# Eight units of the second attention layer on their first twelve key tiles, beside the last dense chain of the first layer

## The chip, the cores and the metric

The kernel runs on one core of one Trainium2 chip. The metric is device time in microseconds of one execution; lower is better. Three executions of the kernel before took 2576.21 to 2576.93 us, median 2576.77 us.

## The reference, cut to what matters

Two layers with the same weights, each one an attention block (32 heads of 16, one shared key and value head) and a dense block, each with a layer norm ahead and a residual sum behind. 2048 rows of 512.

```python
B, S, D, H = 1, 2048, 512, 32;  Dh = 16;  Dff = 1792
q = (x @ wq).reshape(B, S, H, Dh)...;  k = x @ wk;  v = x @ wv
scores = jnp.einsum("bhqd,bkd->bhqk", q, k) * (Dh ** -0.5)
p = _softmax(scores, axis=-1)
o = jnp.einsum("bhqk,bkd->bhqd", p, v)          # then heads joined, @ wo
h = jnp.maximum(jnp.einsum("bsd,df->bsf", x, w1), 0); return jnp.einsum("bsf,fd->bsd", h, w2)

x = x + A(layernorm(x)); x = x + B(layernorm(x))   # layer 0
x = x + A(layernorm(x)); x = x + B(layernorm(x))   # layer 1
```

## The kernel before, in words

**Units and steps.** A layer's rows are four blocks of 512 rows, its heads eight groups of four. A unit is one block with one group: units 0 to 31 are layer 0 (block 0 has units 0 to 7, and so on), units 32 to 63 layer 1. A unit runs over 16 key tiles of 128 keys; one unit on one key tile is a step, so there are 1024 steps. A step has two halves of scores (`scores`, line 709, two concurrent 64-row matmuls into one PSUM tile `st`), an exponential of 128 x 1024 behind each half on ScalarE (line 710), and one product with the values (`values`, line 715) which adds into the PSUM tile `acc`. There is one `acc` tile. When a run of consecutive steps of one unit ends, `keep` (line 718) copies `acc` to a tile `accs` in SBUF, or adds it there if the unit already has a sum. The program holds three tiles `p` of exponentials, so scores can lead products by three steps.

**What must come first.** A step of layer 1 on key tile kt needs the keys of block kt // 4 of layer 1, and those need the residual rows that the chain of layer 0 on that block makes. `chain(L, b)` (line 529) is that dense work: output projection, norm, the two dense products over 14 tiles of the hidden width, and for layer 0 the keys of layer 1 (`keys`, line 289). It can only start when the last unit of block b is done. `front` (line 926) asks for the keys with `until`; where they are not there yet, `until` (line 785) issues all the work that they wait for at once, with no step in between ("forced": full 128-row matmuls, line 98, instead of the 64-row pairs of line 119, and ScalarE takes over copies).

**Order of steps.** `order` (line 813): units 0 and 1 alternate in groups of four key tiles, 2 to 31 run whole, then units 32 and 33 run key tiles 0 to 11, then both run tiles 12 to 15, then 34 to 63 run whole. Step 512 is the first of layer 1.

**Who mixes steps and dense work.** `timed` (line 844) writes TensorE's order ahead of time: after each half of scores it chooses a product, the next scores, or a piece of dense work. How much dense work a step gets is `rate` (line 791): what is left of the work at the head of a list, divided by the steps left to its deadline. `follow` (line 942) puts a chain on the list with its size and its deadline as a step number. The chain of layer 0 on block 3 has size 414 and deadline 531; behind it come the queries of block 3 (`queries`, deadline 575) and those of blocks 1 and 2 (`late`, deadline 640).

**Queries of a unit.** `load_q` (line 663) brings a unit's queries from DRAM (`fqd`) into one of three SBUF tiles `fqop` by two DMAs on SP's queue; `after` (line 971) calls it when unit U has ended, for unit U + 2, behind `unit_out` (the sums' way to DRAM, `fod`). Queries get to DRAM in `queries`: per batch of two groups 12 DMAs of `fqd` (line 370), and per block eight more of `fqr` (line 350). SP's queue carries these, the weights `fw`, the sums (`fod`, `foraw`, `flsum`, `frd`, `frinv`, lines 731 to 754) and the residual rows, in the order of the program.

Of the kernel before, what the change touches and what calls it, by code (L numbers as in the profile page):

```python
# [44 lines left out]
class _Net:  # L45
# [333 lines left out]
    def start(self):  # L379
# [3 lines left out]
        def load(t):  # L383
            xs[t] = self.wt("xt", [P, D], bufs=6)
            self.nc.sync.dma_start(xs[t], self.x[0, t * P:(t + 1) * P, :])
# [44 lines left out]
    def residual(self, L, b):  # L430
        src = self.x[0, b * D:(b + 1) * D, :] if L == 0 else self.xres[b]
        xs = []
        for s in range(4):
            xt = self.wt("xt", [P, D], bufs=6)
            self.nc.sync.dma_start(xt, src[s * P:(s + 1) * P, :])
            xs.append(xt)
        return xs
# [91 lines left out]
    def chain(self, L, b):  # L529
# [33 lines left out]
        if self.early:  # L563
            for s in range(4):
                ps = self.early[s]
                for i, (x, y) in enumerate(self.out_parts(s, 3)):
                    nc.tensor.matmul(ps, x, y, start=False, stop=(i == 2))
                    yield 1.0
                added(s, ps)
                yield from alone(s)  # L570
        else:
            jobs = [([o for G in range(4) for o in self.out_parts(s, G)],
                     lambda ps, s=s: added(s, ps), lambda s=s: alone(s)) for s in range(4)]
            yield from self.batch(*jobs[0:2])
            yield from self.batch(*jobs[2:4])
        yield from self.flip(todo)
# [86 lines left out]
    def load_q(self, U):  # L663
        nc = self.nc
        L, b, u = U // 32, (U // 8) % 4, U % 8
        self.until(lambda: self.haveq[L, b] > u // 2)
        q = self.qop[U % 3]
        r = 48 if self.exact else 49
        for h in range(2):
            nc.sync.dma_start(_f(q)[64 * h:64 * h + r], self.qd[L, b][u, h, 0:r])  # L670
        return q
# [46 lines left out]
    def keep(self, U, acc):  # L718

        if U not in self.sums:  # L720
            self.sums[U] = self.wt("accs", [P, D], bufs=1 if self.exact else 2)
# [35 lines left out]
    def unit_norm(self, U):  # L757
        nc = self.nc
        o, r = self.ol
        G = (U % 8) // 2  # L760
        h, l = self.ot2[0][:, G], self.ot2[1][:, G]
# [51 lines left out]
    def order(self):  # L813
# [4 lines left out]
        out += [(U, kt) for U in (32, 33) for kt in range(12)] + [(U, kt) for U in (32, 33) for kt in range(12, KT)]  # L818
        return out + [(U, kt) for U in range(34, 64) for kt in range(KT)]
# [88 lines left out]
    def run(self):  # L908
        self.normed, self.todo = (1, 3), []
        self.have, self.haveq = [0, 0], {(L, b): 0 for L in range(2) for b in range(NB)}  # L910
        self.gens, self.lag, self.left, self.spent, later = [], 0, 0.0, 0.0, {}
        self.setup()
        self.add(self.start(), 200, 29)
        qs = {U: self.load_q(U) for U in range(2)}
# [6 lines left out]
        steps = self.order()  # L921
        n = len(steps)
        accs, ps, self.sums = {}, {}, {}
        self.first = lambda i: i == 0 or steps[i - 1][0] != steps[i][0]

        def front(i):
# [3 lines left out]
            if self.exact and kt == 0:  # L930
                self.row_max(L, qs[U])
            ps[i] = self.wt("p", [P, 4, D], bufs=3)
            self.scores(U, kt, qs[U], ps[i], 0)

        def back(i):
            U, kt = steps[i]
            self.scores(U, kt, qs[U], ps[i], 1)
# [4 lines left out]
        def follow(L, b):  # L942
            if L == 0 and b == NB - 1:
                self.add(self.chain(L, b), 414, 531)
                self.add(self.queries(1, 3, range(4)), 52, 575)
                self.add(self.late(1, (1, 2)), 114, 640)
            else:
                i0 = 128 * (4 * L + b + 2) + (5 if (L, b) == (0, 2) else 0)
                self.add(self.chain(L, b), (466 if b == 0 else 414) if L == 0 else 390, i0 + (2 if (L, b) != (1, 2) else -6))
# [21 lines left out]
        def after(i):  # L971
            U, kt = steps[i]
            if kt == KT - 1:
                self.unit_out(U)
                if U + 2 < 64:
                    qs[U + 2] = self.load_q(U + 2)
# [100 lines left out]
```

## Time and profile before

| | us |
|---|---|
| median of 3 executions | 2576.77 |
| the profiled execution | 2580.33 |
| its span, first to last instruction | 2578.5 |
| TensorE busy | 2433.6 |
| ScalarE busy | 1992.6 |
| VectorE busy | 722.8 |
| GpSimd busy | 211.9 |

The profiled execution is 1.8 us longer than its span, and 3.6 us longer than the median. A busy time is the union of an engine's instructions; matmuls are pipelined and their ends are modelled, so a busy TensorE is not one at its peak. "PE" is TensorE's matmuls, "PEld" its weight loads, "ACT" ScalarE, "DVE" VectorE, "POOL" GpSimd, "SPq" SyncE's queue of DMA issues.

### The profile page before, as it was taken

The page shows a single profiled execution, that of the slowest core. Times are in us where ns is not written, and L with a number is a line of the kernel's source. Part 1 is how long each engine was busy: PE and PEld are TensorE (multiplying, and loading weights), DVE is VectorE, ACT ScalarE, POOL GpSimd, SP SyncE. Part 2 cuts the span into 40 slices and gives each one's busy share as a digit, 9 for nine tenths or more (in the row PEclk, how much of TensorE's full clock was granted, in tenths as well). Part 3 has the DMA queues.
Part 4 walks back from the last instruction along what each step waited for, and adds up shares of the span by engine and source line. Part 5 has one row for each costly group of instructions (what it writes and reads, how often), then busy time and mean ns, then how long its engine had stood idle before and what let it go on. Part 6 is the DMA issues. An engine that isn't in the chain of part 4 may idle for free.

```text
span 2578.5 us, 44807 instructions
## 1 busy us (share of the span) xinstructions
PE 2433.6 (94%) x18945; PEld 816.8 (32%) x18945; DVE 722.8 (28%) x1554; ACT 1992.6 (77%) x2114; POOL 211.9 (8%) x291
## 2 busy tenths in 40 slices
PE   6898999999999999999898999999999999999978
PEld 2222223333333333333243222233333333333324
DVE  4444423123231132111333132231113121221232
ACT  5487898878888888888542998888898888888830
POOL 2234530000000000000000010000000000000000
PEclk8899999999999999999899999999999999999989
DMA  2034442101311112120221121211112110221031
GB/s 87 22 111 130 131 131 73 52 29 41 98 56 50 40 36 78 41 68 29 82 70 36 48 71 48 86 57 61 35 67 67 56 48 28 77 66 57 21 114 64
DMA packets 110340, 165.12 MB, mean 64 GB/s; under 512 B 19872, under 2 KB 39600, under 8 KB 110128
## 3 DMA queue, kind: packets, MB, share of 16 engines
q1 hardware_dynamic: 110128, 162.16, 19.5%
q8 instruction: 150, 2.46, 0.4%
q14 instruction: 62, 0.51, 0.1%
HBM read 116.20 MB, written 45.88 MB: 63 GB/s over the span
## 4 chain that ended last, share of the span: by engine, by line
PE 77%; ACT 10%; DVE 5%; DMA 3%; issue 2%; POOL 2%; SPq 1%; ACTq 0%; POOLq 0%; DVEq 0%
PE facc L715 32%; PE fmisc L119 20%; PE fst L709 17%; ACT fp L710 10%; PE fmisc L98 7%; DVE fxtl L279 1%; PE fmisc L275 1%; DVE fbst L255 1%; SPq L370 1%; DMA flsum<-fod 1%; DVE fxt L508 1%; DVE fxth L93 1%; POOL fbmv L259 1%; DMA frinv<-frd 0%; DVE fxn L264 0%
## 5 line engine op out<-in xcount | busy, mean ns | idle before, releaser
L710 ACT ACTIVATE fp<-fst 128x1024 f32<-128x1024 f32 x2048 | 1947.7, 1029 | 363.6 <-PE fst L709 345.1
L715 PE MATMUL facc<-fp,fva 128*32 128x512 f32 x8192 | 1038.2, 604 | 11.9 <-DVE faccs L722 11.6
L709 PE MATMUL fst<-fqop,fkop 64*128 64x512 f16 x4096 | 785.2, 383 | 47.0 <-ACT fp L710 33.3
L709 PEld LDWEIGHTS <-fkop 64*128 64x128 f16 x4096 | 257.5, 93 | 875.9 <-issue 728.0
L715 PEld LDWEIGHTS facc<-fp,fva 128*32 128x32 f32 x8192 | 202.6, 108 | 409.5 <-issue 354.3
L119 PE MATMUL fmisc<-fxth,fw 64*128 64x512 f16 x1376 | 237.7, 376 | 2.3 <-DVE fseen L126 1.7
L119 PE MATMUL fmisc<-fw,fhh 64*128 64x512 f16 x1328 | 222.3, 376 | 3.6 <-DVE fseen L126 1.8
L508 DVE SCALAR_TENSOR_TENSOR fxt<-fmisc,fxt 128x512 f32<-128x512 f32 x156 | 103.2, 684 | 370.7 <-PE fmisc L119 319.9
L258 POOL TENSOR_SCALAR fbmv<-fbmv 128x1 f32<-128x1 f32 x84 | 22.2, 264 | 1867.5 <-DVE fbmv L257 1866.1
L126 DVE COPY fseen<-fmisc 1x1 f32<-1x1 f32 x236 | 25.4, 142 | 474.2 <-PE fmisc L119 474.2
L119 PEld LDWEIGHTS <-fw 64*128 64x128 f16 x2064 | 104.7, 94 | 96.1 <-issue 7.2
L119 PE MATMUL fmisc<-fxtl,fw 64*128 64x512 f16 x688 | 132.3, 376 | 0.2
L119 PE MATMUL fmisc<-fw,fhl 64*128 64x512 f16 x664 | 128.5, 376 | 0.0
L722 DVE COPY faccs<-facc 128x512 f32<-128x512 f32 x64 | 44.2, 691 | 275.5 <-PE facc L715 275.5
L587 DVE TENSOR_SCALAR fhh<-fmisc 128x512 f16<-128x512 f32 x84 | 57.6, 686 | 209.5 <-PE fmisc L119 209.5
L585 ACT ACTIVATE fhh<-fmisc 128x512 f16<-128x512 f32 x28 | 16.6, 597 | 100.9 <-PE fmisc L98 95.7
L588 DVE SCALAR_TENSOR_TENSOR fhl<-fmisc,fhh 128x512 f16<-128x512 f32 x112 | 77.4, 692 | 60.6 <-ACT fhh L585 57.7
L119 PEld LDWEIGHTS <-fhh 64*128 64x128 f16 x1328 | 68.8, 94 | 64.4 <-issue 12.8
L275 PE MATMUL fmisc<-fident,fxn 128*128 128x128 f32 x336 | 58.3, 308 | 31.6 <-DVE fxn L264 27.9
L98 PE MATMUL fmisc<-fw,fhh 128*128 128x512 f16 x232 | 69.0, 379 | 0.0
L98 PE MATMUL fmisc<-fxth,fw 128*128 128x512 f16 x208 | 64.1, 385 | 0.7 <-ACT fxth L91 0.7
L255 DVE BATCH_NORM_STATS2 fbst<-fxt 128x6 f32<-128x512 f32 x84 | 57.7, 687 | 17.6 <-DMA fxt<-in_A_x_dram 12.5
(132 smaller groups left out, 1299.8 us busy)
## 6 DMA issues: line engine op xcount, KB each, us to landing
fw<-fwd SPq DMA_DIRECT2D x224, 256.0 KB
fod<-faccs SPq DMA_DIRECT2D x64, 256.0 KB
fqop<-fqd SPq DMA_DIRECT2D x128, 98.0 KB
fxt<-in_A_x_dram SPq DMA_DIRECT2D x44, 256.0 KB
fqd<-fqh SPq DMA_DIRECT2D x128, 64.0 KB
foraw<-fod SPq DMA_DIRECT2D x32, 256.0 KB
frinv<-frd SPq DMA_DIRECT2D x32, 256.0 KB
fwraw<-in_B_w_dram SPq DMA_DIRECT2D x28, 256.0 KB
```

Source lines behind the costliest of these rows:

```text
L93: self.nc.vector.tensor_copy(out, ps)
L98: self.nc.tensor.matmul(ps, a, b, start=(i == 0), stop=(i == n - 1))
L119: mm(ps[j], a[r], b[r], start=(turn == 0 and i == 0), stop=(turn == 1 and i == n - 1), skip_group_check=True)
L255: nc.vector.bn_stats(st, xt)
L275: nc.tensor.transpose(ps[:, c * P:(c + 1) * P], xn[:, c * P:(c + 1) * P], self.ident)
L508: self.nc.vector.scalar_tensor_tensor(xt, ps, 1.0 / factor, xt, op0=MUL, op1=ADD)
L587: nc.vector.tensor_scalar(hh, ps, 0.0, None, op0=MAX)
L588: nc.vector.scalar_tensor_tensor(hl, ps, 0.0, _f(hh), op0=MAX, op1=SUB)
L709: nc.tensor.matmul(st[:, hf], self.kop[U // 32][h, kt * P:(kt + 1) * P], q[h, pr, :], start=True, stop=True)
L710: nc.scalar.activation(p[:, 2 * pr:2 * pr + 2], st, AF.Exp, scale=self.up ** -2)
L715: self.nc.tensor.matmul(acc[32 * j:32 * j + 32], self.va[U // 32][:, kt], p[:, 2 * pr + hf], start=start, stop=stop, skip_group_check=True)
L722: self.nc.vector.tensor_copy(self.sums[U], acc)
```

## The change

Units 32 to 39 now all run key tiles 0 to 11 (96 steps, 512 to 607), then all run tiles 12 to 15 (32 steps, 608 to 639). Their partial sums wait in SBUF, so `accs` has nine tiles. A unit's queries are loaded once for each run, at the end of the run two before it, and ahead of `unit_out`. The last chain of layer 0 gets the deadline 604, and what stands behind it 617, 632 and 648; `late(1, (1, 2))` becomes two entries. The chain of layer 0 on block 2 gets the deadline 510 (it was 519). `unit_norm` does not overwrite the attention output before the chain ahead has read it (`outs`, `asked`). `xt` has eight tiles instead of six.

```diff
-            xs[t] = self.wt("xt", [P, D], bufs=6)
+            xs[t] = self.wt("xt", [P, D], bufs=6 if self.exact else 8)
...
+        self.outs += 1
         yield from self.flip(todo)
...
-        q = self.qop[U % 3]
+        q = self.qop[self.loaded % 3]
+        self.loaded += 1
...
-            self.sums[U] = self.wt("accs", [P, D], bufs=1 if self.exact else 2)
+            self.sums[U] = self.wt("accs", [P, D], bufs=1 if self.exact else 9)
...
+        self.until(lambda: self.outs == self.asked)
...
-        out += [(U, kt) for U in (32, 33) for kt in range(12)] + [(U, kt) for U in (32, 33) for kt in range(12, KT)]
-        return out + [(U, kt) for U in range(34, 64) for kt in range(KT)]
+        out += [(U, kt) for kts in (range(12), range(12, KT)) for U in range(32, 40) for kt in kts]
+        return out + [(U, kt) for U in range(40, 64) for kt in range(KT)]
...
+        self.first = lambda i: i == 0 or steps[i - 1][0] != steps[i][0]
+        units = [steps[i][0] for i in range(n) if self.first(i)]
...
+        qs = {r: self.load_q(units[r]) for r in range(2)}
...
+            self.asked += 1
             if L == 0 and b == NB - 1:
-                self.add(self.chain(L, b), 414, 531)
-                self.add(self.queries(1, 3, range(4)), 52, 575)
-                self.add(self.late(1, (1, 2)), 114, 640)
+                self.add(self.chain(L, b), 414, 604)
+                self.add(self.queries(1, 3, range(4)), 52, 617)
+                self.add(self.late(1, (1,)), 57, 632)
+                self.add(self.late(1, (2,)), 57, 648)
             else:
-                i0 = 128 * (4 * L + b + 2) + (5 if (L, b) == (0, 2) else 0)
-                self.add(self.chain(L, b), (466 if b == 0 else 414) if L == 0 else 390, i0 + (2 if (L, b) != (1, 2) else -6))
+                early = {(0, 2): 2, (1, 2): 6}.get((L, b), -2)
+                self.add(self.chain(L, b), (466 if b == 0 else 414) if L == 0 else 390, 128 * (4 * L + b + 2) - early)
...
+            r = run_of[i] + 2
+            if (i + 1 == n or self.first(i + 1)) and r < len(units):
+                qs[r] = qs[r - 2] if units[r] == U else self.load_q(units[r])
             if kt == KT - 1:
                 self.unit_out(U)
-                if U + 2 < 64:
-                    qs[U + 2] = self.load_q(U + 2)
```

What the change does to the order is seen at three places.

**TensorE, where the last chain of layer 0 runs.** Before, at step 535: the last scores (`fst`), three products in a row (`facc`, x12), and behind them dense rows alone (`fw` weights, `fmisc` PSUM) until the keys are there, 324 of them full matmuls of line 98.

```order
L709 MATMUL fst_13017<-fqop_89,fkop_76 128x512
L709 LDWEIGHTS fkop_76
L709 MATMUL fst_13017<-fqop_89,fkop_76 128x512
L715 MATMUL facc<-fp,fva_78 32x512 x12
L119 LDWEIGHTS fw_12564
L119 MATMUL fmisc<-fxth,fw_12564 128x512
L119 LDWEIGHTS fw_12568
```

After, at step 550, in unit 35's first run (line 711 is 709 before, 717 is 715):

```order
L119 LDWEIGHTS fw_13164
L119 MATMUL fmisc<-fxtl,fw_13164 128x512
L711 LDWEIGHTS fkop_76
L711 MATMUL fst_13395<-fqop_91,fkop_76 128x512
L711 LDWEIGHTS fkop_76
L711 MATMUL fst_13395<-fqop_91,fkop_76 128x512
L717 MATMUL facc<-fp,fva_78 32x512 x12
L711 LDWEIGHTS fkop_76
L711 MATMUL fst_13413<-fqop_91,fkop_76 128x512
L711 LDWEIGHTS fkop_76
L711 MATMUL fst_13413<-fqop_91,fkop_76 128x512
L119 LDWEIGHTS fw_13168
```

The dense rows now stand between the two halves of a step's scores and behind them, and products come in groups of up to three. In all the order has 68, 100, 136, 128, 148, 188, 96 and 96 rows of line 119 in the eight stretches of 16 steps from 512 on, where it had 78, 104, 34, 24, 36, 60, 28 and 64 and the 324 full ones; the chain ends in step 607 with 16 rows of line 119, 16 transposes and the 12 matmuls of `keys` that no step stands between. From 640 to 767 it has 828 rows of line 119, where it had 736.

**SyncE's queue, in the runs of four steps.** Before, from the end of the second query batch of block 3 (`fqd13`) on, the next queries loaded (`fqop1`) are for a run that begins 16 steps later:

```order
L370 DMA fqd13_100<-fqh_14244 4x16x512 x2
L370 DMA fqd13_100<-fql_14245 4x16x512
L370 DMA fqd13_100<-fqh_14244 4x16x512
L350 DMA fqd13_100<-fqr_14317 4x512 x8
L435 DMA fxt_14327<-fxr1_102 128x512
L435 DMA fxt_14329<-fxr1_102 128x512
L435 DMA fxt_14331<-fxr1_102 128x512
L435 DMA fxt_14333<-fxr1_102 128x512
L731 DMA fod_14070<-faccs_14352 128x512
L670 DMA fqop1_90<-fqd10_97 49x1024 x2
```

After, from the end of the same batch on:

```order
L370 DMA fqd13_100<-fql_15277 4x16x512
L370 DMA fqd13_100<-fqh_15276 4x16x512
L672 DMA fqop2_91<-fqd10_97 49x1024 x2
L733 DMA fod_15304<-faccs_13380 128x512
L350 DMA fqd13_100<-fqr_15325 4x512 x8
L435 DMA fxt_15335<-fxr1_102 128x512
L435 DMA fxt_15337<-fxr1_102 128x512
L435 DMA fxt_15339<-fxr1_102 128x512
L435 DMA fxt_15341<-fxr1_102 128x512
L754 DMA frd_15356<-flsum_15239 128x32
L756 DMA frinv_15358<-frd_15356 128x1x512
L672 DMA fqop0_89<-fqd10_97 49x1024 x2
```

`fqop2` here holds the queries of unit 36, whose run begins at step 624, four steps behind the last matmul of the batch; `fqop0` those of unit 37 for step 628. The queries of unit 34, for step 616, stand in the same way behind the first batch, which ends in step 612.

**SyncE's queue, before unit 40.** In step 637 the order now has the second half of block 1's queries forced (24 rows of line 119 and four of line 343 with no step between), since the load of unit 40's queries asks for them. After:

```order
L370 DMA fqd11_98<-fqh_15794 4x16x512 x2
L370 DMA fqd11_98<-fql_15795 4x16x512
L370 DMA fqd11_98<-fqh_15794 4x16x512
L350 DMA fqd11_98<-fqr_15811 4x512 x8
L672 DMA fqop0_89<-fqd11_98 49x1024 x2
L733 DMA fod_15823<-faccs_14535 128x512
```

`fqop0` is unit 40's, for step 640. Before, block 1's queries went to DRAM 24 steps and more before that step.

## Rows read from the trace of the kernel before

**Rows 1.** the page, part 1: busy us (share of the span) and instructions of each engine
```profile
PE 2433.6 (94%) x18945; PEld 816.8 (32%) x18945; DVE 722.8 (28%) x1554; ACT 1992.6 (77%) x2114; POOL 211.9 (8%) x291
```

**Rows 2.** the page, part 5: the exponentials of a step on ACT
```profile
L710 ACT ACTIVATE fp<-fst 128x1024 f32<-128x1024 f32 x2048 | 1947.7, 1029 | 363.6 <-PE fst L709 345.1
```

**Rows 3.** busy time by stretch: PE, PEld, DVE, ACT, POOL, granted clock, DMA share, GB/s
```profile
982.70:1259.30 276.60, 260.44 (x2127) 89.91 (x2123) 69.27 (x152) 215.28 (x229) 8.27 (x17) 0.97 0.14 45
1259.30:1614.90 355.60, 337.42 (x2357) 109.07 (x2357) 99.81 (x195) 256.09 (x275) 24.89 (x43) 0.98 0.19 61
1614.90:1898.10 283.20, 275.98 (x2296) 91.04 (x2297) 62.17 (x137) 243.12 (x256) 5.43 (x10) 1.00 0.17 55
1235.70:1257.90 22.20, 12.40 (x47) 5.61 (x45) 11.76 (x26) 3.95 (x6) 4.34 (x8) 0.71 0.09 36
1315.60:1386.70 71.10, 70.49 (x342) 31.80 (x339) 22.16 (x36) 8.25 (x14) 1.13 (x3) 1.00 0.25 81
1386.70:1403.00 16.30, 8.83 (x34) 4.16 (x33) 9.46 (x19) 2.98 (x5) 3.79 (x6) 0.79 0.09 35
```

**Rows 4.** four stretches of 16 steps each, dense matmuls of line 119 alone
```profile
427.94:465.24 37.30, 18.18 (x135) 6.53 (x132) 1.00 0.27 85
1583.40:1614.90 31.50, 9.57 (x66) 3.04 (x62) 1.00 0.13 41
1930.50:1966.30 35.80, 9.58 (x72) 3.35 (x68) 1.00 0.14 43
1966.30:2001.50 35.20, 15.08 (x114) 5.46 (x110) 1.00 0.27 90
```

**Rows 5.** the third of them, transposes of line 275 alone
```profile
1930.50:1966.30 35.80, 2.41 (x16) 1.70 (x16) 1.00 0.14 43
```

**Rows 6.** chain of waits, 1185 to 1230 us: start, us, what: value products
```profile
1190.96 2.71 PE facc L715 x24
...
1196.48 0.99 PE facc L715 x8
```

**Rows 7.** chain of waits, whole span: key matmuls, a query load's landing, a sums load's landing
```profile
1246.11 4.86 PE fmisc L98 x11
...
1553.67 5.91 DMA fqop<-fqd
...
1560.57 3.67 DMA flsum<-fod
```

**Rows 8.** timeline, the first pause: start, us, engine, line, tiles [idle before <-releaser]
```profile
1251.05 0.60 ACT L91 ACTIVATE fkv<-fmisc 128x512 f32<-128x512 f32 x1 [5.72 <-PE fmisc L98]
...
1257.91 1.73 PE L709 MATMUL fst<-fqop,fkop 64*128 64x512 f16 x4 [2.65 <-DMA fkop<-fqr]
...
1259.31 1.94 ACT L710 ACTIVATE fp<-fst 128x1024 f32<-128x1024 f32 x2 [7.67 <-PE fst L709]
```

**Rows 9.** timeline of SP's queue, 1543 to 1561 us: DMA issues of one query batch
```profile
1544.59 0.52 SPq L370 DMA_DIRECT2D fqd<-fqh  x1
...
1551.81 0.52 SPq L370 DMA_DIRECT2D fqd<-fqh  x1
...
1553.28 0.90 SPq L670 DMA_DIRECT2D fqop<-fqd  x2
1554.28 5.55 SPq L350 DMA_DIRECT2D fqd<-fqr  x8
```

**Rows 10.** waits on the value products' PSUM tile, whole span: us, times
```profile
  PEld facc L715: 26.0, 40
  PE facc L715: 11.6, 6
```

**Rows 11.** timeline, 1560 to 1590 us: VectorE waits for a landing, TensorE for VectorE
```profile
1564.25 0.42 DVE L748 SCALAR_TENSOR_TENSOR fgood<-flsum,fgood 128x32 f32<-128x32 f32 x2 [3.63 <-DMA flsum<-fod]
...
1567.19 0.39 PE L119 MATMUL fmisc<-fxth,fwqh 64*128 64x512 f16 x2 [2.65 <-DVE fxth L93]
```

**Rows 12.** by line: the squares of the queries on POOL
```profile
L366 POOL TENSOR_TENSOR fsq<-fqh 128x512 fp32r<-128x512 f16 x32 | 33.2, 1039 | 242.7 <-DVE fqh L93 238.8 <-ACT fqh L91 3.9
```

More of the change, by code (lines that the diff above doesn't have):

```diff
@@ L433, in residual @@
         for s in range(4):
-            xt = self.wt("xt", [P, D], bufs=6)
+            xt = self.wt("xt", [P, D], bufs=6 if self.exact else 8)
             self.nc.sync.dma_start(xt, src[s * P:(s + 1) * P, :])
@@ L911, in run @@
         self.gens, self.lag, self.left, self.spent, later = [], 0, 0.0, 0.0, {}
+        self.outs = self.asked = 0
         self.setup()
         self.add(self.start(), 200, 29)
-        qs = {U: self.load_q(U) for U in range(2)}
+        steps, self.loaded = self.order(), 0
+        n = len(steps)
+        self.first = lambda i: i == 0 or steps[i - 1][0] != steps[i][0]
+        units = [steps[i][0] for i in range(n) if self.first(i)]
+        run_of = [0] * n
+        for i in range(1, n):
+            run_of[i] = run_of[i - 1] + self.first(i)
+        qs = {r: self.load_q(units[r]) for r in range(2)}
         self.until(lambda: self.haveq[0, 0] > 0)
@@ L920, in run @@
             self.until(lambda: self.tile_no >= 5)
-        steps = self.order()
-        n = len(steps)
         accs, ps, self.sums = {}, {}, {}
-        self.first = lambda i: i == 0 or steps[i - 1][0] != steps[i][0]
         def front(i):
@@ L930, in front @@
             if self.exact and kt == 0:
-                self.row_max(L, qs[U])
+                self.row_max(L, qs[run_of[i]])
             ps[i] = self.wt("p", [P, 4, D], bufs=3)
-            self.scores(U, kt, qs[U], ps[i], 0)
+            self.scores(U, kt, qs[run_of[i]], ps[i], 0)
         def back(i):
             U, kt = steps[i]
-            self.scores(U, kt, qs[U], ps[i], 1)
+            self.scores(U, kt, qs[run_of[i]], ps[i], 1)
         def at(i, fn, *a):
```

## The prediction, made before the changed kernel ran

> **What bounds the kernel now.** I read the page first: TensorE is busy for 94% of the span, ScalarE for 77% [rows 1, 2], so over the whole kernel TensorE is the scarce engine. An average hides stages, so next I read the stretch around the change in windows [rows 3]: steps 400 to 511 (982.7 to 1259.3 us), 512 to 639 (to 1614.9) and 640 to 767 (to 1898.1). TensorE's busy time falls short of these three by 16.2, 18.2 and 7.2 us, 41.6 in all. Two pauses without any exponential stand out. From 1235.7 to 1257.9 ScalarE has 4.0 us of work and TensorE 12.4 of 22.2: the end of chain (0, 2), which step 512 waits for. From 1315.6 to 1386.7 TensorE is busy 70.5 of 71.1 us with chain (0, 3) alone, while ScalarE has 8.3; behind it stand 16.3 us of its tail (norm, transposes, keys) with TensorE at 8.8. So the chain stops the steps for 87 us, but TensorE does work in most of that. What can be won is not 87 us: the same matmuls must go into steps that cost more for it.
>
> How much more, undisturbed stretches of 16 steps tell [rows 4]. With 64 rows of line 119 (66 counted, two being cut at the edges) they take 31.5 us, with 114 35.2, with 134 37.3. Between 64 and 134 a row costs 5.8 / 70 = 0.083 us. The 71.1 us window holds 324 full matmuls and 13 pairs, 0.21 us each, so 0.105 us for one row of a pair; that is what I take for a row above 134, where TensorE alone sets the pace. 16 transposes cost extra: 35.8 us with 64 rows and 16 of them [rows 4, 5], 4.3 more than without.
>
> **The change part by part.** The counts of rows are those of the order shown above.
>
> *Steps 512 to 639.* By these prices the eight stretches take 31.8, 38.8 (100 rows, 16 transposes), 37.5, 36.8, 38.8 (134 rows and 14 at 0.105), 59.3, 34.2 and 38.5 us. The 59.3 is 41.3 for 172 rows, 1.7 for the last 16 rows that stand alone, and the tail of 16.3 [rows 3], which the order still has between steps 607 and 608. Sum 315.7 against 355.6: **-39.9 us**. It comes from steps which before ran with 24 to 64 rows, bound by ScalarE with TensorE in part idle, and from products that now go in twos and threes.
>
> Here a rule of the Trainium skill speaks against mixing. A row shows first that three products in a group take 2.71 us, and one takes 0.99 [rows 6], so a group of three saves 0.26 over three single ones, 0.13 for each change of kind. "TensorEngine Tiling (Array Packing)", Key Properties, says that changing the tiling mode drains the engine; the 71.1 us of the chain alone have no product between them, so by the rule alone the moved chain would cost more. By the row the order's groups of products decide: 205 in steps 512 to 767 before, 147 after, so 58 x 0.13 = 7.5 us are given back, and they are already in the prices above [rows 4].
>
> *Steps 640 to 767* have 828 rows for 736: 38.5 + 34.2 + 37.3 + 35.7 + 34.8 + 36.0 + 35.0 + 35.5 = 287.0 against 283.2, **+3.8 us**.
>
> *Steps 400 to 511.* Of the first pause, what is ahead of the copy of the keys at 1251.05 (15.4 us) goes, since the order has the keys' matmuls inside step 511; the 6.9 us from there to the scores at 1257.91 stay [rows 8]. Back into the steps come 24 rows (2.0), 16 transposes (4.3) and 12 full matmuls (2.5): **-6.6 us**.
>
> *Six more runs* (78 for 72). The waits for the one `acc` tile are 37.6 us over 46 times [rows 10], 0.82 each: **+4.9 us**. The eight sums that are added instead of copied (VectorE is busy for 28% [rows 1]), the nine `accs` tiles and eight `xt` tiles are taken at nothing: no wait for such a tile stands among the rows I read, and if the cover on VectorE is gone, it is in the waits below.
>
> So far -37.8 us. Against it stand **new waits**, all on SyncE's queue, which issues in order. With runs of four steps a unit's queries are loaded some four steps before their use, and the order puts two of these loads right behind 12 DMAs of a query batch. The row of such a batch [rows 9]: first issue 1544.59, last ends 1552.33, 7.7 us; the two `fqop` issues start at 1553.28 and the second lands 5.91 us behind its issue at 1553.67 [rows 7], 6.3 us together. With the copy out of PSUM ahead (0.6 on ScalarE for the keys [rows 8], taken as 0.7) the queries are there 14.8 us after the batch's last matmul. If the landing took 3.7 us, like that of the sums' load [rows 7], it would be 12.6.
> - Step 616: three steps lie between (3 x 34.2 / 16 = 6.4 us). Wait 6.2 to 8.4; I take 7, nearer the row that stood behind such a batch.
> - Step 624: four steps without dense work (4 x 31.5 / 16 = 7.9). Wait 4.7 to 6.9; I take 5.5.
> - Step 640: the forced half batch, 0.7 for the copy, 7.7 for 12 issues, 5.6 for eight `fqr` [rows 9], 4.1 to 6.3 for the load, 18 to 20.3 us. TensorE's work against it is two and a half steps (4.9); the squares on POOL, 2 x 1.04 [rows 12], lie inside. Loss 13 to 15.4; I take 14.
> - VectorE: it waits 3.63 us for a landing of sums, and TensorE 2.65 us for VectorE [rows 11]. With four pairs of units ending in 32 steps this can come none to four times (0 to 10.6 us); I take 4, one and a half.
>
> Together 30.5 us; the ends are none at all (if everything is early) and about 58 (below). A page names a smaller price: "DMA: Bandwidth & Descriptors", Anatomy of one DMA, puts the fixed cost of a DMA at about 2.0 us and says that a semaphore wait is held by the issuing sequencer. The trace agrees with the second (the queue stands in order [rows 9]). By an estimate with 2.0 for 5.9 the three query waits would be 3.9 us less each, 18.8 instead of 30.5 together, and the time 2558; the row decides here.
>
> **Sum.** -39.9 + 3.8 - 6.6 + 4.9 + 30.5 = -7.3 us. Against the profiled execution (2580.33, span 2578.5 and 1.8 around it) that gives 2573.0; the median of the three executions is 3.6 us lower, so the same sum from 2576.8 gives **2569.5 us**.
>
> **Rivals.**
> 1. *The queue is early.* If scores reach steps 616, 624 and 640 later than I think, or loads land sooner, the waits shrink to some 6 us. For it: VectorE and the queue have free time, SyncE's work of the 32 steps is less than their length. Against it: the order puts `fqop` behind the whole batch. 2576.8 - 37.8 + 6 = 2545.
> 2. *Slower: every short run waits.* Units 34 to 39 start at six steps, 616 to 636, each four steps behind the issue of its queries, and the same queue carries for each pair `fod`, `foraw`, `flsum`, `frd` and `frinv`, two of which wait for a landing. If all six wait 5.5 us, and VectorE is held at all four pairs (10.6), the waits are 33 + 14 + 10.6 = 57.6 and the time 2576.8 - 37.8 + 57.6 = 2597. It decides once the waits pass 37.8 us. For it: each wait delays the sums' DMAs behind it. Against it: after 624 no query batch lies ahead of a load until 640.
> 3. *Nothing is won.* If TensorE, not ScalarE, is the limit of the light steps too, a row costs 0.105 us from 64 on. The 380 or so rows above 64 in steps 512 to 639 then cost 8.4 us more, and those of 640 to 767 about 1: -37.8 + 9.4 + 30.5 = +2, 2579. For it: only 41.6 us of idle time stand in the three stretches. Against it: the stretch with 114 rows, 35.2 us, lies below the line of 0.083.
>
> The clock can add to any of them: in the first pause the granted clock was 0.71 and in the second 0.79 [rows 3], and eleven of the keys' matmuls took 4.86 us [rows 7], 0.44 each for 0.21, the lower of the two levels (1.2 for 2.4 GHz). Both tails stay, so this stays too; a new wait of several us may bring 2 us of it more.
>
> **How the numbers follow.** Forecast 0.42, rival 1 0.17, rival 2 0.24, rival 3 0.17. 0.2%, 5.2 us, is about what a measurement can tell from no change. The forecast's own range is 2563 to 2580 (each wait at its ends, 23.9 to 41.3 us), two thirds and more of it beyond that bound: 0.34 of its 0.42 count as faster, with rival 1 0.51. Rival 3 lies on both sides of no change and takes 0.16 into the middle, 0.24 with the rest of the forecast; slower is 0.25. The range leaves out the far half of rivals 1 and 2: 2548 to 2592.
>
> **What would show it.** Right: no stretch without exponentials from 1315 to 1387 us; steps 544 to 606 at 2.3 to 2.7 us each; a tail of some 16 us behind step 607; TensorE's scores released by `fqop` at the starts of units 34, 36 and 40, together some 25 us; steps 400 to 767 at about 908 us for 915.4. Wrong: `fqop` releases scores less than 5 us in all (rival 1), or at every run from 616 to 636 (rival 2); or steps 544 to 591 above 2.5 us each without any wait (rival 3).

## The result, and the profile after

The changed kernel takes 2585.76 us (median of 7 executions, 2582.67 to 2591.27), the kernel before 2576.85 beside it (7 executions, 2574.81 to 2579.56): a ratio of 1.0039, 95% interval 1.0026 to 1.0052. It is 0.39% slower; 2569.5 and "faster" had been forecast. The profiled execution is at the top of its range, 2591.27 with a span of 2589.5.

The page of the changed kernel, part 1 and the exponentials of part 5, which answer to [rows 1, 2]:

```profile
PE 2425.4 (94%) x19269; PEld 829.8 (32%) x19269; DVE 740.8 (29%) x1606; ACT 1979.6 (76%) x2098; POOL 212.3 (8%) x291
...
L712 ACT ACTIVATE fp<-fst 128x1024 f32<-128x1024 f32 x2048 | 1944.1, 1029 | 460.1 <-PE fst L711 437.1
```

TensorE works 8.2 us less than before over the whole span, yet ScalarE waits 92 us more for scores (437.1 for 345.1). Windows tell where. Columns as in [rows 3]; steps 400 to 511, 512 to 639, 640 to 767, and by itself the part 608 to 655:

```profile
984.74:1252.13 267.39, 255.16 (x2131) 89.62 (x2127) 72.55 (x158) 212.36 (x226) 8.27 (x17) 0.99 0.15 47
1252.13:1614.03 361.90, 325.05 (x2577) 115.65 (x2576) 98.46 (x210) 246.43 (x264) 19.81 (x33) 0.94 0.19 60
1614.03:1909.58 295.55, 287.38 (x2395) 98.65 (x2398) 78.12 (x168) 242.74 (x257) 10.63 (x20) 0.99 0.18 59
...
1504.48:1656.41 151.93, 125.57 (x903) 41.73 (x901) 55.83 (x114) 93.33 (x98) 18.81 (x28) 0.89 0.30 96
```

Against [rows 3] steps 400 to 511 gain 9.2 us, 512 to 639 lose 6.3 and 640 to 767 lose 12.4. (The two spans differ by 1.5 us more than these steps; step 400 begins 2.0 us later in the changed kernel, and ahead of it the two programs are alike.) In steps 512 to 767 TensorE is busy for 612.4 us; before it was 613.4. Its time without work grew from 25.4 to 45.0 us, about the 18.6 that these steps lost. That its busy time hardly fell is in part the lower granted clock of steps 512 to 639 (0.94 for 0.98); in number 9 below, at 0.97, it is 603.2.

The waits of steps 608 to 642 on DMAs (what waits <- for what: us in total, times, longest), 1500 to 1620 us:

```profile
DVE fbst L255 <- DMA fxt<-fxr: 25.5, 3, 13.4
PEld L711 <- DMA fqop<-fqd: 15.8, 3, 6.0
PE fst L711 <- DMA fqop<-fqd: 15.1, 5, 5.5
```

And three places in the timeline. SyncE's queue: the first and the last issue of a query batch, the load of unit 34's queries behind them, and 30 us on the residual rows of block 1:

```profile
1517.88 0.58 SPq L370 DMA_DIRECT2D fqd<-fqh  x1
...
1524.72 0.52 SPq L370 DMA_DIRECT2D fqd<-fqh  x1
1525.35 1.61 SPq L672 DMA_DIRECT2D fqop<-fqd  x2
...
1556.40 2.85 SPq L435 DMA_DIRECT2D fxt<-fxr  x4
```

TensorE at steps 616, 624, 625 and 640, with its idle time ahead and what ended it, and VectorE between the second and the third:

```profile
1530.63 1.15 PE L711 MATMUL fst<-fqop,fkop 64*128 64x512 f16 x2 [5.46 <-DMA fqop<-fqd]
...
1554.94 0.39 PE L711 MATMUL fst<-fqop,fkop 64*128 64x512 f16 x1 [4.32 <-DMA fqop<-fqd]
...
1559.48 0.69 DVE L255 BATCH_NORM_STATS2 fbst<-fxt 128x6 f32<-128x512 f32 x1 [11.55 <-DMA fxt<-fxr]
...
1562.33 1.09 PE L275 MATMUL fmisc<-fident,fxn 128*128 128x128 f32 x4 [3.12 <-DVE fxn L264]
...
1612.33 0.61 PE L711 MATMUL fst<-fqop,fkop 64*128 64x512 f16 x1 [4.70 <-DMA fqop<-fqd]
```

Each wait begins in SyncE's queue: 7.5 us of issues stand ahead of unit 34's load, and its scores, those of step 616, start 5.28 us after that load was issued. The same happens for unit 36 (step 624), for the residual rows (VectorE idle, then the transposes, late), and for unit 40.

### The profile page after: what moved, and what is told of

It is laid out like the page before. It is cut to its first block, busy times and chain, and to the rows that moved or that the text cites. A ratio compares the mean times of both kernels' runs of the same rounds, so it can differ in the third digit from the quotient of the medians.

```text
span 2589.5 us, 45442 instructions
## 1 busy us (share of the span) xinstructions
PE 2425.4 (94%) x19269; PEld 829.8 (32%) x19269; DVE 740.8 (29%) x1606; ACT 1979.6 (76%) x2098; POOL 212.3 (8%) x291
## 4 chain that ended last, share of the span: by engine, by line
PE 78%; ACT 10%; DVE 4%; DMA 3%; issue 2%; POOL 2%; SPq 1%; ACTq 0%; POOLq 0%; DVEq 0%
PE facc L717 33%; PE fmisc L119 22%; PE fst L711 17%; ACT fp L712 9%; PE fmisc L98 4%; PE fmisc L275 1%; SPq L370 1%; DVE fxtl L279 1%; DVE fbst L255 1%; POOL fbmv L259 1%; DMA fod<-faccs 0%; DVE fxth L93 0%; DVE fxt L508 0%; DMA fwd<-fw 0%; DMA fxt<-fxr 0%
## 5 line engine op out<-in xcount | busy, mean ns | idle before, releaser
L712 ACT ACTIVATE fp<-fst 128x1024 f32<-128x1024 f32 x2048 | 1944.1, 1029 | 460.1 <-PE fst L711 437.1
L717 PE MATMUL facc<-fp,fva 128*32 128x512 f32 x8192 | 1029.5, 605 | 11.1 <-DVE faccs L724 10.8
L119 PE MATMUL fmisc<-fxth,fw 64*128 64x512 f16 x1568 | 275.4, 376 | 1.7 <-DVE fseen L126 0.9
L119 PE MATMUL fmisc<-fw,fhh 64*128 64x512 f16 x1568 | 260.9, 376 | 4.6 <-DVE fseen L126 2.1
L119 PEld LDWEIGHTS <-fw 64*128 64x128 f16 x2352 | 119.0, 94 | 114.7 <-issue 10.8
L119 PE MATMUL fmisc<-fxtl,fw 64*128 64x512 f16 x784 | 152.2, 376 | 0.1
L119 PE MATMUL fmisc<-fw,fhl 64*128 64x512 f16 x784 | 152.2, 376 | 0.0
L588 DVE TENSOR_SCALAR fhh<-fmisc 128x512 f16<-128x512 f32 x98 | 67.2, 686 | 238.2 <-PE fmisc L119 238.1
L119 PEld LDWEIGHTS <-fhh 64*128 64x128 f16 x1568 | 81.1, 94 | 81.7 <-issue 21.2
L275 PEld LDWEIGHTS fmisc<-fident,fxn 128*128 128x128 f32 x336 | 40.8, 156 | 57.2 <-DVE fxn L264 30.3
L469 POOL TENSOR_SCALAR fwraw<-fwraw 128x512 f32<-128x512 f32 x32 | 48.3, 1508 | 74.3 <-DVE fw L468 55.3
L264 DVE TENSOR_SCALAR fxn<-fxt,fbmv 128x512 f32<-128x512 f32 x84 | 45.5, 542 | 29.4 <-POOL fbmv L259 29.2
```

The costliest lines, as they stand in the source:

```text
L119: mm(ps[j], a[r], b[r], start=(turn == 0 and i == 0), stop=(turn == 1 and i == n - 1), skip_group_check=True)
L264: self.nc.vector.tensor_scalar(xn, xt, mv[:, 0:1], mv[:, 3:4], op0=SUB, op1=MUL)
L275: nc.tensor.transpose(ps[:, c * P:(c + 1) * P], xn[:, c * P:(c + 1) * P], self.ident)
L469: nc.gpsimd.tensor_scalar(raw, raw, self.ws, None, op0=MUL)
L588: nc.vector.tensor_scalar(hh, ps, 0.0, None, op0=MAX)
L712: nc.scalar.activation(p[:, 2 * pr:2 * pr + 2], st, AF.Exp, scale=self.up ** -2)
```

## The experiments

Step times below are differences between the starts of the steps' first exponentials in the profiled executions. Line numbers differ by one or two between kernels.

**1. Only the earlier deadline.** The kernel before with chain (0, 2) due at step 510, nothing else:

```diff
-                i0 = 128 * (4 * L + b + 2) + (5 if (L, b) == (0, 2) else 0)
+                i0 = 128 * (4 * L + b + 2) - (4 if (L, b) == (0, 2) else 0)
```

> The kernel before with one edit: the chain of layer 0 on block 2 has the deadline 510 instead of 519. Theory (this part of the change wins what the changed profile shows from steps 400 to 512, 9.2 us): 2567 to 2570 us. Rival (the work moved into the steps costs as much as the pause): 2575 to 2579.

Measured: 2566.64 us, ratio 0.9964 (0.9949 to 0.9979), at the lower end of the theory. Its windows, steps 400 to 511 and 512 to 639:

```profile
980.77:1248.17 267.40, 255.15 (x2131) 89.64 (x2127) 72.50 (x158) 212.36 (x225) 8.27 (x17) 1.00 0.15 47
1248.17:1602.57 354.40, 336.96 (x2366) 109.24 (x2366) 99.84 (x195) 255.87 (x276) 24.89 (x43) 0.98 0.19 62
```

One line, and the whole gain of steps 400 to 511, with the others as before [rows 3]. So the changed kernel wins only in the part that has nothing to do with the eight units, and with them it is 19 us slower than this one (2585.8 for 2566.6).

**2. The eight units alone.** The counterpart: the changed kernel with chain (0, 2) due at 519.

```diff
-                early = {(0, 2): 2, (1, 2): 6}.get((L, b), -2)
+                early = {(0, 2): -7, (1, 2): 6}.get((L, b), -2)
```

> The changed kernel with chain (0, 2) due at step 519 again, as before the change: the eight units alone. If the two parts of the change add up, the pause behind step 511 comes back (steps 400 to 511 about 9 us longer), 2585.8 + 10 = about 2596 (2592 to 2600). If the early end of chain (0, 2) only helps where steps 512 on are as full as before the change, 2585 to 2590.

2594.17 us, 1.0061 (1.0047 to 1.0076). Step 511 takes 24.2 us again for 11.0. The two parts add up within the noise: 16.7 us lost with the eight units (2594.2 for the 2577.5 of the kernel before beside it), 8.4 of them won back with the deadline.

**3. No second load of queries.** The changed kernel with eight `qop` tiles, so that a unit's queries stay from its first run to its second.

```diff
-        self.qop = [self.ct(f"qop{i}", [P, 2, D], self.pt) for i in range(3)]
+        self.qop = [self.ct(f"qop{i}", [P, 2, D], self.pt) for i in range(3 if self.exact else 8)]
...
-                qs[r] = qs[r - 2] if units[r] == U else self.load_q(units[r])
+                seen = units.index(units[r])
+                qs[r] = qs[seen] if seen < r else self.load_q(units[r])
```

> The changed kernel with eight query tiles, so that units 32 to 39 keep their queries from the first run to the second and nothing is loaded again; all else as changed. Theory A (the new waits stand behind the query loads on SyncE's queue): the waits of 6.1 us at step 616 and 5.6 at 624 go, those at 626 and 637 to 640 stay, 11 to 12 us less than the changed kernel, about 2574. Rival B (the time went into the steps' own matmuls, and SyncE's queue only fills the gap): within 4 us of the changed kernel.

2577.9 us, 1.001 (0.9995 to 1.0025), for the 2574 of theory A: the loss is nearly made good. Step 615 takes 1.82 us for 8.11, step 623 3.04 for 7.60. But the waits at steps 625 and 637 to 640 stay (9.36 and 25.9 us, 6.36 and 27.1 in the changed kernel), since other loads cause them. Windows, steps 608 to 655:

```profile
1504.51:1645.05 140.54, 120.29 (x903) 41.54 (x901) 56.00 (x114) 92.90 (x99) 18.70 (x28) 0.91 0.30 95
```

The same 903 matmuls take TensorE 5.3 us less than in the changed kernel: without the two waits its granted clock is higher.

**4. Issue or landing?** The changed kernel, the loads for units 34 to 40 issued from GpSimd's queue.

```diff
+        queue = nc.gpsimd if not self.exact and 34 <= U <= 40 else nc.sync
         for h in range(2):
-            nc.sync.dma_start(_f(q)[64 * h:64 * h + r], self.qd[L, b][u, h, 0:r])
+            queue.dma_start(_f(q)[64 * h:64 * h + r], self.qd[L, b][u, h, 0:r])
```

> The changed kernel, and the query loads of units 34 to 40 are issued by GpSimd, whose queue has no other DMA, instead of SyncE. It tells the order of issue from the landing. If the waits at steps 616 and 624 come from the place in SyncE's queue behind the 12 DMAs of a query batch, the loads of units 36 and 38 leave some 7 us earlier and land before their steps: steps 615 and 623 at about 2 us instead of 8.1 and 7.6, in all 8 to 11 us less than the changed kernel, 2575 to 2578. If the landing is slow because the batch's DMAs are under way, they stay within 2 us of what they were, 2583 to 2588. Against both: GpSimd's own work (the squares of the query batch) may hold the issue, then the wait moves but stays.

2583.4 us, 1.0024 (1.0015 to 1.0033). The time lies in the range of the second theory (the landing is slow), and its interval overlaps that of the changed kernel; by itself it would speak against the place in the queue. The steps don't: 615 takes 2.69 us and 623 3.06. (By the order above, the loads for steps 616 and 624 are those of units 34 and 36; the expectation calls them 36 and 38.) Steps 625 and 626 took 4.5 us more than in the changed kernel, so part of the gain went again. GpSimd's issue, and TensorE's wait for unit 34, 5.46 us before:

```profile
1515.38 2.14 POOL L673 DMA_DIRECT2D fqop<-fqd  x4
...
1521.12 0.37 PE L712 MATMUL fst<-fqop,fkop 64*128 64x512 f16 x1 [0.60 <-DMA fqop<-fqd]
```

SyncE issues the batch from 1513.03 to 1521.66 us, so the load leaves in the middle of it, and it takes no less time than before (5.74 us from issue to scores). Only the place in the issuing queue differs. So the two waits come from the order of issue.

**5, 6. Block 1's queries earlier.** The forced half batch at steps 637 to 640 goes if `late(1, (1,))` runs long before. First behind chain (0, 1), due by 402; then that with block 2's queries behind chain (0, 2) as well, due by 526, and the queries kept in SBUF.

```diff
-                self.add(self.late(1, (1,)), 57, 632)
...
+                if (L, b) == (0, 1):
+                    self.add(self.late(1, (1,)), 57, 402)
```

> The changed kernel with the queries of block 1 of layer 1 taken out of steps 624 to 637 and put behind chain (0, 1), deadline 402; queries of units 32 to 39 are still loaded twice. Theory A: the forced stretch and the wait at steps 637 to 640 (19 us in the changed profile) and the wait for residual rows at 626 (4.4) go, those at 616 and 624 stay: 18 to 24 us less than the changed kernel, 2562 to 2568. Rival B: the same dense work stands elsewhere, within 5 us of the changed kernel.

> The changed kernel with the queries kept in SBUF, the queries of block 1 behind chain (0, 1) and those of block 2 behind chain (0, 2). Theory A: no new wait is left but parts of the tail behind step 607: 35 us and more below the changed kernel, 2540 to 2552, so below both. Rival B: not below 2570.

2594.52 us, 1.0069 (1.0043 to 1.0094), slower than the changed kernel, a miss; and 2575.66, 0.9999 (0.9984 to 1.0015). Steps 384 to 511 of the first take 323.1 us, 301.1 in the changed kernel:

```profile
949.48:1272.61 323.13, 301.31 (x2495) 108.27 (x2494) 99.44 (x215) 244.13 (x260) 17.14 (x30) 0.99 0.18 57
```

The 57 rows and 16 transposes brought forward cost 22 us there: TensorE is busy for 13 us more (301.3 for 288.2), and it stands for 9 us more, in part because chain (0, 2), pushed back by them, got its pause again (step 511: 15.5 us for 11.0). In the second no wait of those named is left in steps 608 to 640, and it is 10 us faster than the changed kernel, yet no faster than the kernel before: of the 54 us that steps 608 to 767 give back (351.2 for 405.1), the earlier rows take 38 in steps 384 to 607.

**7, 8. Block 1's queries where steps are light.** Steps 512 to 518 of the changed kernel have almost no dense work. With the queries in SBUF, `late(1, (1,))` stands behind chain (0, 2), due by 526; in the other, ahead of chain (0, 3), due by 536.

```diff
-                self.add(self.late(1, (1,)), 57, 632)
...
+                if (L, b) == (0, 2):
+                    self.add(self.late(1, (1,)), 57, 526)
```

> The kernel with the queries kept in SBUF, and the queries of block 1 of the second layer are made right behind chain (0, 2) (due by step 526) instead of behind chain (0, 3) (due by 632). Steps 512 to 518 have almost no dense work after the change, so this is where it should fit. Theory A (the waits at steps 625 and 637 to 640 are the rest of what was lost): nothing is forced between steps 637 and 640, and steps 608 to 655 take about 111 us instead of the 140.5 of the kernel with the queries in SBUF (in the run with both blocks early they took 102, with block 2's rows gone as well); steps 512 to 606 take 6 to 8 us more for the 57 rows and 16 transposes. 2577.9 - 29.5 + 7 = about 2556 (2550 to 2563). Theory B (dense work beside full steps costs its full price wherever it goes, as with block 1 at step 402, which paid 20 us for it): 2570 to 2578.

> As the kernel before it in this call, but the queries of block 1 are made between the end of chain (0, 2) and chain (0, 3), due by step 536: the same work later by some ten steps, in steps that chain (0, 3) needs as well, so that the chain ends later (102 full-size rows of it are left to run alone behind step 607, for 24 full rows there in the other). Theory A: the same gain at 608 to 655, but 7 to 10 us paid behind step 607, 2557 to 2566 and not faster than its neighbour. Theory B: 2572 to 2582.

2573.96 us, 0.9985 (0.9973 to 0.9997), and 2584.61, 1.0025 (1.0015 to 1.0034). The order of the two came as expected, but the times of theory A, 2556 and 2557 to 2566, were far too low; the first lies in the range of theory B, the second above it. In the first, steps 637 to 640 fall from 25.9 to 17.5 us and step 627 rises to 11.2; in the second step 607, with the chain's rest, takes 37.8 us for 19.3. The waits of the first, 1500 to 1620 us, and its queue at two places:

```profile
DVE fbst L255 <- DMA fxt<-fxr: 9.6, 1, 9.6
PEld L710 <- DMA fqop<-fqd: 7.6, 1, 7.6
PE fst L710 <- DMA fqop<-fqd: 6.7, 1, 6.7
```

```profile
1557.91 1.76 SPq L435 DMA_DIRECT2D fxt<-fxr  x4
...
1596.75 1.20 SPq L671 DMA_DIRECT2D fqop<-fqd  x2
```

Now the residual rows of block 2 and unit 40's queries stand behind a batch: here moving a batch changed which load is caught.

**9. No load behind a batch.** Number 7 with those two loads issued earlier:

```diff
+            at(600, lambda: self.rows.update({(1, 2): self.residual(1, 2)}))
+            for c in range(2):
+                at(612 + 4 * c, lambda U: ahead.update({U: self.load_q(U)}), 40 + c)
```

> The kernel with block 1's queries in the gap at step 512, and the two loads that still came behind a batch of queries are issued earlier: the residual rows of block 2 (in that kernel the steps stand 9 us at 627 for them) at step 600, and the queries of units 40 and 41 (8 us at 639) at steps 612 and 616. No instruction is taken away. If the place in SyncE's queue is the cause, steps 627 and 639 take 2 to 3.5 us each and the time is 2574.0 - 9 - 7 = about 2558 (2554 to 2563). If the landing or the work behind them is the limit, the steps stay over 8 us and the time within 3 us of 2574.

2561.36 us, 0.9942 (0.9921 to 0.9963), 3.4 above the 2558 and inside its range. Step 627 takes 2.00 us, steps 637 to 640 8.36 together. Nothing was taken out of the program, these loads came 20 steps and more earlier, and 12.6 us went. Windows, steps 512 to 639 and 640 to 767, and what still waits for a DMA (1500 to 1620 us):

```profile
1248.39:1594.11 345.72, 324.12 (x2625) 115.77 (x2626) 111.80 (x234) 245.72 (x262) 24.89 (x43) 0.97 0.19 61
1594.11:1876.45 282.34, 279.04 (x2334) 94.05 (x2331) 64.33 (x142) 242.97 (x256) 5.43 (x10) 1.00 0.18 57
```

```profile
DVE foraw L764 <- DMA frinv<-frd: 12.5, 3, 6.2
DVE fgood L749 <- DMA flsum<-fod: 6.4, 2, 4.7
```

**10. The price of runs.** The changed kernel with units 48 to 51 split in the same way, where no batch is issued:

```diff
-        return out + [(U, kt) for U in range(40, 64) for kt in range(KT)]
+        out += [(U, kt) for U in range(40, 48) for kt in range(KT)]
+        out += [(U, kt) for kts in (range(12), range(12, KT)) for U in range(48, 52) for kt in kts]
+        return out + [(U, kt) for U in range(52, 64) for kt in range(KT)]
```

> The changed kernel, and units 48 to 51 run on the first twelve key tiles and then on the last four as well, in a place (steps 768 to 831) where no query batch is issued and no chain ends: the price of runs by itself, four more of them. By the prediction's 0.82 a run, steps 768 to 831 take about 3.3 us more than the 139.2 of the changed kernel (32.34, 35.82, 35.10, 36.86 in its stretches of 16, less what begins in them by chance), 2 to 5. If each short run also waits for its queries (rival 2), four units with 4 to 6 us each: 16 us or more.

(The four numbers in it add up to 140.1; 139.2 was a slip.) Steps 768 to 831, this kernel and then the changed one:

```profile
1902.98:2043.68 140.70, 138.26 (x1152) 44.95 (x1146) 36.11 (x78) 121.75 (x130) 3.36 (x8) 1.00 0.22 73
```

```profile
1909.58:2049.69 140.11, 137.81 (x1150) 44.79 (x1143) 34.85 (x75) 121.80 (x130) 3.36 (x8) 1.00 0.20 67
```

0.6 us for four runs, 0.15 each (one execution), not 0.82, and no wait for queries: both theories stated were too high. The same steps take 139.4 to 140.4 us in the other kernels, so 0.15 can't be told from nothing.

**11. The price of a row in full steps.** The changed kernel; chain (0, 3) leaves out the product of the hidden values' low half with the second weight matrix, 112 rows of line 119.

```diff
-                    (hs[f][0][:, t], w[1, f][0]), (hs[f][0][:, t], w[1, f][1]), (hs[f][1][:, t], w[1, f][0]))],
+                    (hs[f][0][:, t], w[1, f][0]), (hs[f][0][:, t], w[1, f][1]), (hs[f][1][:, t], w[1, f][0]))[:2 if (L, b) == (0, 3) and not self.exact else 3]],
...
-                self.add(self.chain(L, b), 414, 604)
+                self.add(self.chain(L, b), 350, 604)
```

> The changed kernel, and chain (0, 3) leaves out the third product of its second weight matrix (the low half of the hidden values by the high half of the weights), so part of the result is not computed; the planner is given 350 instead of 414 for its size, so that it still ends at step 607. By the order, line 119 has 656 rows in steps 512 to 607 instead of 768, most of the 112 missing ones in steps 576 to 607. What a row costs in full steps can be read from it: by the prediction's law (0.083 up to 134 in 16 steps, 0.105 above) the six stretches get 10 to 11.5 us shorter than the changed kernel's 252.4, 241 to 242; if TensorE is the limit all along and a row costs what line 119's own busy time gives (21.00 us for 158 rows, 0.133), 14 to 15 us, 237.5 to 238.5; if something else held these steps (ScalarE, PSUM), under 8 us.

Steps 512 to 607, the changed kernel, then this one:

```profile
1252.13:1504.48 252.35, 239.33 (x1978) 87.94 (x1979) 64.69 (x140) 183.71 (x197) 8.26 (x17) 0.97 0.15 49
```

```profile
1252.09:1495.23 243.14, 227.33 (x1858) 80.62 (x1859) 65.90 (x142) 182.95 (x196) 8.29 (x17) 0.97 0.16 50
```

9.2 us (one execution), 0.082 a row; TensorE's busy time falls by 12.0. That lies between the first theory (10 to 11.5) and the third (under 8), a little nearer the first, and far from the second. The slope of the prediction's law, 0.083, holds; the dearer row above 134 does not show.

**12. The last wait.** Number 9, and for units 32 to 37 the inverse sums (`frd`, `frinv`) go by GpSimd's queue.

```diff
+        queue = nc.gpsimd if not self.exact and 32 <= U < 38 else nc.sync
-        nc.sync.dma_start(rd.rearrange("h (c x) -> h c x", x=32), l[:, 1])
+        queue.dma_start(rd.rearrange("h (c x) -> h c x", x=32), l[:, 1])
```

> The kernel without a load behind a batch, and for units 32 to 37 the write and the read of the inverse sums are issued by GpSimd instead of SyncE. In the kernel before it step 629 takes 7.6 us: VectorE stands 3.3 us for the inverse sums, whose DMAs come behind a query batch on SyncE's queue, and the transposes' copies stand behind it. If that place in the queue is the cause, step 629 takes 3.5 to 4.5 us, the time 2558 (2554 to 2562); the difference is too small for the runs, the step tells. If GpSimd's wait for the first landing holds its small operations of the norm, another step between 624 and 640 gets longer by as much.

2560.31 us, 0.9935 (0.9916 to 0.9955), not to be told from number 9. Step 629 falls from 7.62 to 6.02 us only, for 3.5 to 4.5 expected; what else holds it was not tried.

## Why the prediction was wrong

Steps 400 to 767 were forecast at 908.1 us and took 924.8 in the profiled execution. By its own terms:

| term | forecast | measured |
|---|---|---|
| steps 400 to 511, against before | -6.6 | -9.2 |
| steps 512 to 607, without waits and run ends | 243.0 | 252.4 with run ends |
| steps 608 to 655, without waits | 111.2 | 117.9 |
| new waits | 30.5 | 34.0 at most |
| steps 656 to 767 | 248.5 | 253.2 |
| six more runs | 4.9 | in the rows above; 0.9 at 0.15 each |

(Waits measured: what steps 615, 623, 625 and 637 to 640 take above the same steps of a kernel in which they don't wait: 6.3 against number 3; 4.6 against number 3; 4.4 and 18.7 against number 9. 117.9 is 151.9 less these. Number 9 does block 1's rows elsewhere, so 4.4 and 18.7 hold some of that work too, and 117.9 is too low by as much. All together the waits are worth 29.4 us: steps 512 to 767 take 657.5 us in the changed kernel and 628.1 in number 9.)

**The new waits** were right in place and cause, and near in size: 6.3 for the 7 at step 616, 4.6 for 5.5 at 624, at most 18.7 for 14 at 637 to 640. The fourth, 4.4 for the 4 "VectorE", came from the residual rows, not from the sums; that its size fits is luck. TensorE's idle time that `fqop` ends is 15.1 us in all, not the 25 that the prediction gave as a sign; in step 616, right behind the first wait, it works for all of the 2.99 us at a granted clock of 0.50. The price of a load, 6.3 us from its first issue [rows 7, 9], was a little high at steps 616 and 624, where the scores start 5.28 and 4.92 us after it, and far too high at 640: 2.50 us, for the 4.1 to 6.3 assumed. The Trainium skill, "DMA: Bandwidth & Descriptors", Anatomy of one DMA, puts the fixed cost at about 2.0 us, in a section on DMAs that GpSimd issues; the load for 640 comes near it, the other two show more, and so does GpSimd's own load in number 4 (5.74). That the queue and not the landing is the cause was argued in the prediction and is shown by numbers 4 and 9.

**Steps 400 to 511** came out near, -9.2 for -6.6, and for the reason given; of the 8.8 us for work put back into the steps, steps 400 to 495 show 4.7 (221.9 for 217.2).

**The step that failed is "Sum 315.7 against 355.6: -39.9 us"**, the term for steps 512 to 639. With steps 640 to 767 (+3.8) and the run ends (+4.9) the prediction had 512 to 767 gain 31.2 us before any wait. Number 9, which has none of the four waits, gains 10.8 there (628.1 for 638.8). So the eight units are worth 11 us in these steps, not 31, and waits of 29.4 us turned that round.

The reason given for the sum, that steps 512 to 639 were "bound by ScalarE with TensorE in part idle", is not what failed. Steps 560 to 575 of the kernel before have 24 rows of line 119, steps 592 to 607 60; columns as in [rows 3]:

```profile
1450.41:1481.40 30.99, 30.50 (x222) 7.56 (x219) 4.04 (x6) 30.57 (x33) 2.08 (x2) 1.00 0.11 35
1514.20:1545.52 31.32, 31.32 (x256) 8.33 (x256) 5.19 (x10) 30.83 (x32) 2.96 (x3) 1.00 0.13 41
```

With 36 rows more they take 0.33 us more, and ScalarE is busy for all but half a microsecond: up to some 60 rows a row is nearly free. In full steps it costs 0.082 (number 11). So the slope was no error. The error was the level. The stretches from which the law was read [rows 4] were taken for their length and their rows of line 119, and their total busy time was not looked at. Two of the three on the line are these:

```profile
1583.40:1614.90 31.50, 31.50 (x258) 8.38 (x254) 3.58 (x7) 30.96 (x32) 2.08 (x2) 1.00 0.13 41
427.94:465.24 37.30, 37.30 (x327) 13.76 (x324) 11.77 (x24) 30.10 (x33) 0.00 (x0) 1.00 0.27 85
```

They are stretches without any loss, at a clock of 1.00. The sum priced every new step like them, and set it against a measured 355.6 us that holds its losses. The changed steps have losses too. Steps 528 to 591, forecast at 151.9 us, have 4.6 us without work:

```profile
1287.28:1444.32 157.04, 152.45 (x1314) 57.66 (x1311) 36.17 (x75) 120.30 (x129) 1.68 (x4) 1.00 0.13 41
```

And the 16 steps behind a tail are dear. In number 9 they are steps 512 to 527 (74 rows and 16 transposes, 36.6 us by the law) and 608 to 623 (96 rows, 34.2 by the law); the last line is step 608 alone:

```profile
1248.40:1289.70 41.30, 37.32 (x289) 12.61 (x290) 17.61 (x37) 30.65 (x33) 5.19 (x10) 0.96 0.34 112
1512.20:1552.60 40.40, 38.94 (x301) 13.05 (x300) 9.93 (x21) 30.36 (x32) 4.16 (x4) 0.93 0.19 62
...
1512.17:1516.71 4.54, 4.54 (x21) 0.88 (x22) 0.58 (x1) 1.94 (x3) 0.00 (x0) 0.50 0.00 0
```

These two are 4.7 and 6.2 us above the law, and the wait at step 629 puts steps 624 to 639 5.5 above it: together 16.4 of the 20.4 us by which number 9 misses the sum. In step 608 TensorE is busy all the time, at half its clock. This split is read from the windows; no run took the tails' price away by itself.

A check against TensorE's busy time would have warned. For steps 512 to 767, without waits, the prediction summed 315.7 + 287.0 = 602.7 us. In the kernel before TensorE's busy time there is 337.4 + 276.0 = 613.4 [rows 3], 605.9 after the 7.5 us that fewer changes of kind were to save. Busy time is no fixed amount of work, but in number 9 it came to 603.2 us. So the forecast left TensorE no time to stand, though the tail alone has 7.5 us of that (16.3 less 8.8, [rows 3]). Number 9 has 24.9 us without work (4.5 of them in step 629), as much as before. The Trainium skill, "TensorEngine Tiling (Array Packing)", Key Properties, says that a change of the tiling mode drains the engine; TensorE's busy time, 10.2 us shorter in number 9 with 160 groups of products for 206, agrees with it.

**The six runs** were mis-sized. The waits for `acc` [rows 10] were divided by their count and taken for the price of a run. In the changed kernel, with 78 runs, the same view shows no more of them, 36.5 us over 44 times for 37.6 over 46:

```profile
  PEld facc L717: 25.4, 38
  PE facc L717: 11.1, 6
```

**The rivals.** Rival 2 gave the side, not the way: the waits (34.0 at most) stayed under its point of 37.8, and the scores of steps 620, 628, 632 and 636, which it has wait too, do not wait (the steps ahead of them take 1.8 to 2.4 us). Rival 3's 2579 came nearest, but its mechanism is not what the runs show: its 0.105 a row from 64 on is 0.082 in number 11, and its sign, steps 544 to 591 above 2.5 us each, is not met (2.44). 2585.8 is inside the range, which was wide for the wrong reason.

**The clock** was put at "2 us more". In steps 608 to 655 it is 0.89, for 0.98 in the same steps before. 903 matmuls take TensorE 125.6 us (139 ns each); in number 9, at a clock of 0.95, 813 take 105.8:

```profile
1512.17:1626.11 113.94, 105.83 (x813) 33.78 (x814) 39.44 (x83) 91.51 (x97) 11.43 (x16) 0.95 0.27 85
```

That is 130 ns each; 9 ns by 903 gives 8 us as an estimate, with the mix of matmuls not quite the same. It can hold the 6.7 us of steps 608 to 655 in the table; no run shows that by itself.

**The better version** is number 9, with or without 12: 0.994 of the time of the kernel before. Number 1, one line, is at 0.9964, and the intervals of the two overlap; whether the eight units with all their repairs beat the one line stays open (9.2 us in the profiled executions for steps 400 to 767, 895.4 against 904.6).

## What to carry to other kernels

Before a gain from mixing two kinds of work is summed up, look at what the price list was read from: stretches without any idle time, at the full clock, price the best case, and a measured time that holds its losses is not to be set against it. Compare the sum with the busy time of the engine that must do both, and ask what pauses it leaves. When runs get shorter, go through every load that the queue issues between a run's announcement and its start: a load that stood 16 steps ahead and is now four steps ahead is late if one batch stands before it. Here moving the batch moved the wait to the next load, and issuing the loads earlier removed it. And measure the parts of a change singly: here one line won 10 us, and the rest of the change lost 19.

## What the runs showed of the hardware

The price of a wait goes on after it. At step 638 of the changed kernel, behind 4.9 us in which TensorE stood for 2.5, three products in a row ran thus (chain and timeline show 2.71 us for the same 24 matmuls elsewhere [rows 6]):

```profile
1601.95 5.15 PE L717 MATMUL facc<-fp,fva 128*32 128x512 f32 x24
```

In the window of just these the granted clock is 0.53, near the lower of its two levels (1.2 for 2.4 GHz). The columns are PE, PEld, clock, DMA share and GB/s:

```profile
1601.95:1607.10 5.15, 5.14 (x24) 0.98 (x24) 0.53 0.26 71
```

Step 608 of number 9, behind the tail of the chain, shows the same: 4.54 us at a clock of 0.50, for the 1.8 to 2.0 us of a step with little dense work.

And the end of a run, with its copy or sum out of the one `acc` tile, cost 0.15 us in number 10, no more than the same steps differ between kernels; it was expected to cost five times that.
